# A scale from sums of the weights in place of a maximum over the products, its reduction first on GpSimd, and four early score blocks in place of eight

## The chip, the cores and the metric

The kernel runs on one core of one Trainium2 chip. The metric is the device time of one execution in microseconds (us); runs of one kernel agree within about 0.1% here (three runs before: 1170.21 to 1171.33). In the profile PE is TensorE (PEld its weight loads), DVE is VectorE, ACT is ScalarE, POOL is GpSimd and SP is SyncE, whose queue issues most DMAs. Each engine works through its own instructions in order.

## The reference

Two branches are added to a residual. With xn the layer norm of x (2048 tokens, 512 features):

```
A: y = Re(DFT_seq(DFT_hidden(xn)))          # dense DFT matrices, given as inputs
B: q  = xn @ w_q                            # 32 heads, two halves of 128 each
   s1 = q1 @ k1.T ; s2 = q2 @ k2.T          # 64 keys each
   top 2 of s1, top 2 of s2 -> 4 candidate sums -> top 2, softmax g
   act = gelu(xn . u[expert])               # 4096 experts
   out = sum g * act * v[expert]
result = x + A(xn) + B(xn)
```

The kernel never forms q. It multiplies w_q with the keys first (the "key products" M, one matrix of 512 x 512 for each chunk of four heads, eight chunks), and then xn with M to get the scores.

## The kernel before, in words

The program is written with a tile framework whose scheduler sets the order of instructions on each engine from the program order, its own costs and the dependencies. Buffers come from pools with a fixed number of slots; a tile in a reused slot waits until the last reader of the slot is done.

**Opening (up to about 90 us).** The tokens come in four groups of 512, in the order G = 1, 0, 2, 3. For each group `ln` (L328 to L367) computes the statistics and normalises, `fold` (L400 to L404) adds tokens that the DFT's symmetry pairs, giving Q[0][g], and `main(0, g)` (L435) multiplies it with a part of the DFT matrix into four PSUM banks of the tag `pa`. These are the "main sums". `evict(0)` (L487, L490) copies the four banks out on ACT, one row of the input (row 512, tile x5, handled on POOL by L367 and `fold_row`, `spread`, L409 to L422) entering as the bias s5c. Then `fold(1, g)` and `main(1, g)` do the second main sum in the same four banks, in the order 0, 1, 2, 3. `stage` (L503 to L505) splits the normalised tokens into two float16 parts and transposes them by DMA, through three staging slots. `sides` (L440 to L473) does some vectors on DVE and POOL.

**The key products of chunk 0** are made in the same stretch. `m_mul` (L148) multiplies w_q's chunk with the keys in float32, in two batches, into the banks `pc` and `pb`. `m_scale` (L187 to L212) then reads the four product tiles on ACT for sums of absolute values, two more sums over one tile of w_q and over the keys, reduces the three numbers over the partitions on POOL (`pow2`, L118, PARTITION_ALL_REDUCE) and makes powers of two from them on DVE: the scale of M[0] (L206, L207), and those of w_q, of the keys and of later chunks. `m_parts` (L219 on ACT, L220 on DVE) writes M[0] as a high and a low float16 part. With it `early(b)` (L266 to L271) computes score blocks: a score block is 128 tokens x 512 scores, 12 matmuls (`s_mm`, L245). Blocks 0 to 3 of the order TO (tokens of group 1) come after `main(0, 0)`, blocks 4 to 7 (tokens of group 0) after `main(1, 1)`; the first four are copied to SBUF (L271), the others stay in the four banks of `pb` and `pc`.

**Score stage.** For each chunk j and each of 16 token blocks `scores` runs the block (unless it is there already), copies it to a slot `ss` (four slots, L817 on ACT), and takes the top values and their places on DVE (L821, L825). Amid it the next chunk's M is built: the loads of chunk 1's w_q are issued by POOL (`m_load`, L134), and their first slots lie in memory that the opening has used; `m_prep` splits each tile in two float16 parts (L158, L163 on ACT; L166 on POOL or L160 on DVE), and stages 1 to 6 of `m_stage` multiply and split it at the blocks that MST0 (chunk 0) and MST name. `m_fit` (L185) sums the absolute values of a finished M for a check at the end. `sums` and `y_rows` (L509 to L521) finish the DFT's hidden side.

**Expert stages.** The rest of the time goes to the products with u (L945) and v (L1028) and what selects and weighs them (L973 to L999), with checks of the inputs beside them and a verdict at the end.

At the very start POOL makes an identity matrix, two iotas and three converted tables from them (`ident`, `iof`, `io_lam`, `io_c`, `hoff`, L72 to L104), which later stages read.

Of the kernel before, what the change touches and what calls it, by code (L numbers as in the profile page):

```python
# [19 lines left out]
P = 128  # L20
# [15 lines left out]
def tile_fnet_peer(ctx, tc, x, ca, cb, c5, wt, wf, wr, wq, kt, ut, vn, out):  # L36
# [33 lines left out]
    cst = ctx.enter_context(tc.tile_pool(name="cst", bufs=1))  # L70
    ident = cst.tile([P, P], F32, name="ident")
    make_identity(nc, ident)  # L72
    io_lam = cst.tile([P, P], F16, name="io_lam")
    io_c = cst.tile([P, NC], F16, name="io_c")
    with tc.tile_pool(name="iop", bufs=1, side="right") as iop:
        iof = iop.tile([P, P], F32, name="iof")
        nc.gpsimd.iota(iof, pattern=[[1, P]], base=0, channel_multiplier=0,
                       allow_small_or_imprecise_dtypes=True)
        nc.gpsimd.tensor_copy(io_lam, iof)
        nc.gpsimd.tensor_scalar(io_c, iof[:, :NC], float(P), None, op0=ALU.mult)  # L80
    eps = cst.tile([P, 1], F32, name="eps")
# [6 lines left out]
    nc.vector.memset(one, 1.0)  # L88
    nc.gpsimd.tensor_scalar(not0, ident[:, 0:1], -1.0, 1.0, op0=ALU.mult, op1=ALU.add)
    flag = cst.tile([1, 1], I32, name="flag")  # L90
    NW = 4 * (NCH - 1)
    NF = NW + 32 + NCH - 1
    sums_sb = cst.tile([P, 139 + NF + 3], F32, name="sums")
    chk, asum = sums_sb[:, 0:71], sums_sb[:, 71:139]


    wsc = cst.tile([P, 5], F32, name="wsc")
    sw, sk, smx, inv1 = wsc[:, 0:1], wsc[:, 1:2], wsc[:, 2:3], wsc[:, 3:4]
# [15 lines left out]

    def pow2(mx, pool, name, w=1):

        m = pool.tile([P, 4, w], F32, tag=f"pow2_{w}", name=name, bufs=2 if w == 1 else 1)
        nc.gpsimd.partition_all_reduce(m[:, 0], mx, P, bass_isa.ReduceOp.absmax)  # L118
        nc.vector.tensor_scalar(m[:, 1], m[:, 0], 1e-30, None, op0=ALU.max)
# [48 lines left out]
    def m_stage(j, pool, stage):  # L168

        if stage == 0:  # L170
            m_load(j, pool, range(4))
        elif stage < 5:
            m_mul(j, stage - 1, range(KD))
        elif stage == 5 and (j, 0, "h") in MS:
            M[j] = MP[j % 2].tile([P, 2, KD, 512], F16, tag="m", name=f"m{j}"), inv1
            MS[j, "s"] = smx
            if j > 1:
                m_fit(j - 1, M[j][0])
        elif stage == 5:
            m_scale(j, MS[j, "p"])  # L180
        else:
            m_parts(j, MS[j, "p"])

    def m_fit(j, junk):
        nc.scalar.activation(junk[:, 0], M[j][0][:, 0], AF.Abs, accum_out=fits[:, NW + 31 + j:NW + 32 + j])  # L185

    def m_scale(j, pm, at=None):  # L187

        if at is not None:
            nc.vector.tensor_copy(at, one)  # L190
        mp = MP[j % 2]
        w = 1 if at is None else 3
        mx = mp.tile([P, KD + w], F32, tag="mx" if w == 1 else "mx3", name=f"mx{j}")
        m = mp.tile([P, 2, KD, 512], F16, tag="m", name=f"m{j}")
        for kd in range(KD):
            nc.scalar.activation(m[:, 0, kd, :], pm[kd], AF.Abs, scale=1.0 if at is None else at,
                                 accum_out=mx[:, kd:kd + 1])
        if w == 3:
            nc.scalar.activation(m[:, 0, 0:2].rearrange("p k n -> p (k n)"),
                                 MS[j, 3].rearrange("p h k -> p (h k)"), AF.Abs, accum_out=mx[:, KD + 1:KD + 2])  # L200
            nc.scalar.activation(m[:, 0, 0, 0:P], k_sb.rearrange("p w k -> p (w k)"), AF.Abs,
                                 accum_out=mx[:, KD + 2:])
        nc.vector.tensor_reduce(mx[:, KD:KD + 1], mx[:, :KD], axis=AX.X, op=ALU.max)
        p, q = pow2(mx[:, KD:], mp, f"pw{j}", w)
# [3 lines left out]
        if w == 3:  # L208
            nc.vector.tensor_scalar(wsc[:, 0:2], q[:, 1:3], 2.0 ** 12, None, op0=ALU.mult)
            nc.vector.scalar_tensor_tensor(wsc[:, 4:5], p[:, 1:2], 2.0 ** -26, p[:, 2:3], op0=ALU.mult, op1=ALU.mult)  # L210
            nc.vector.scalar_tensor_tensor(smx, q[:, 0:1], 2.0 ** 11, wsc[:, 4:5], op0=ALU.mult, op1=ALU.mult)
            nc.vector.tensor_scalar(inv1, p[:, 0:1], 2.0 ** -12 / XS, None, op0=ALU.mult)  # L212
        M[j] = m, sc[:, 1:2]
        MS[j, "s"] = sc[:, 0:1]

    def m_parts(j, pm):
# [362 lines left out]
    for g in GK[1]:  # L579
# [64 lines left out]
    def part_b(safe, stS, stP, stE, xt, u_sb, cmp_p):  # L644
# [825 lines left out]
```

## Time and profile before

| what | value |
|---|---|
| median of three runs | 1170.43 us (1170.21 to 1171.33) |
| the profiled execution | 1170.59 us |
| its span, first to last instruction | 1168.8 us |
| PE busy | 1133.7 us (97%) |
| DVE busy | 934.9 us (80%) |
| ACT busy | 607.4 us (52%) |
| POOL busy | 247.8 us (21%) |
| mean granted TensorE clock | 0.988 |

A line of the time line has the start in us, the length, engine, source line, operation, output <- inputs with their shapes, the number of instructions merged into it, and in square brackets how long the engine stood idle before it and what ended that ("issue": nothing that the profile shows). A line of the waits has who waited for whom, the total in us, how often, and the longest. A line of a group has the total time, the mean of one in ns, and the idle time before. Float32 matmuls appear twice in the counts of PE.

### The profile page before, as it was taken

How to read it: one execution, taken by the hardware profiler on the slowest of the kernel's cores; microseconds unless marked ns; L12 is line 12 of the kernel's file. 1: busy time of each engine (PE TensorE's matmuls, PEld its weight loads, DVE VectorE, ACT ScalarE, POOL GpSimd, SP SyncE). 2: the span in 40 equal slices, each digit the busy share in tenths (PEclk: the TensorE clock that was granted, in tenths of full speed). 3: DMA queues.
4: the chain of work that ended last, by engine and by line, in shares of the span. 5: the costliest groups of instructions: out<-in, count | busy, mean ns of one | idle time of the engine just before them, and what ended most of it. 6: DMA issues, size and time to landing. Idle time of an engine off the chain costs nothing.

```text
span 1168.8 us, 25265 instructions
## 1 busy us (share of the span) xinstructions
PE 1133.7 (97%) x9858; PEld 720.1 (62%) x9858; DVE 934.9 (80%) x2848; ACT 607.4 (52%) x1050; POOL 247.8 (21%) x235
## 2 busy tenths in 40 slices
PE   5598999999999999999999999999999999999997
PEld 4244655445445449868469569569559659658763
DVE  7698788798898999983995886787886887788670
ACT  5537667777776754353535436535535436434440
POOL 5222636757757330000010010010000000000000
PEclk9798899999999999999999999999999999999999
DMA  9477055342341203260643644545545455442423
GB/s 338 123 168 265 31 173 177 109 163 91 108 160 40 91 26 109 84 223 11 213 171 130 200 155 158 184 158 171 178 161 176 166 171 167 154 154 68 142 73 103
DMA packets 98400, 167.83 MB, mean 144 GB/s; under 512 B 32980, under 2 KB 48219, under 8 KB 98270
## 3 DMA queue, kind: packets, MB, share of 16 engines
q1 hardware_dynamic: 97328, 163.94, 43.1%
q0 software_dynamic: 640, 2.10, 0.5%
q8 instruction: 79, 1.29, 0.5%
q14 instruction: 51, 0.42, 0.1%
q10 hardware_dynamic: 302, 0.08, 0.0%
HBM read 142.69 MB, written 17.63 MB: 137 GB/s over the span
## 4 chain that ended last, share of the span: by engine, by line
PE 75%; DVE 15%; POOL 4%; issue 2%; DMA 2%; ACT 1%; POOLq 0%; SPq 0%; DVEq 0%; ACTq 0%
PE v L1028 27%; PE z L945 26%; PE s L245 15%; PE g L983 4%; DVE vals L821 4%; DVE idx L825 3%; PE m L144 1%; PE p L435 1%; POOL wq L165 1%; DVE L L973 1%; POOL wq L166 1%; DVE z L763 1%; DVE act L999 1%; DMA wq<-in_wq_dram 1%; DVE ft L400 1%
## 5 line engine op out<-in xcount | busy, mean ns | idle before, releaser
L945 PE MATMUL z<-xb,u 128*128 128x256 f16 (+1 forms) x3840 | 342.7, 251 | 0.0
L1028 PE MATMUL v<-v,act 128*128 128x512 f16 x1536 | 338.6, 379 | 0.0
L945 PEld LDWEIGHTS <-u 128*128 128x128 f16 x3840 | 309.4, 98 | 26.8
L245 PE MATMUL s<-m,xq 128*128 128x512 f16 x1344 | 301.7, 383 | 11.8 <-DVE m L220 11.8
L1028 PEld LDWEIGHTS <-act 128*128 128x128 f16 x1536 | 147.1, 98 | 171.2
L245 PEld LDWEIGHTS <-xq 128*128 128x128 f16 x1344 | 130.5, 99 | 166.0 <-issue 17.8
L973 DVE TENSOR_TENSOR L<-io_lam,cmp 128x2048 f16<-128x2048 f16 x128 | 155.9, 1218 | 59.2 <-PE g L983 59.0
L952 ACT ACTIVATE act<-z,scl 128x256 f32<-128x256 f32 (+1 forms) x224 | 100.8, 498 | 169.2 <-PE z L945 169.1
L1041 POOL TENSOR_TENSOR y<-y,xr 128x512 f32<-128x512 f32 x15 | 25.3, 1685 | 613.7 <-DMA y<-y_d 393.5
L821 DVE MAX8 vals<-ss 128x8 f32<-128x64 f32 x896 | 133.5, 217 | 5.0 <-ACT ss L817 4.7
L998 ACT ACTIVATE act<-w 128x1024 f16<-128x1024 f32 x52 | 69.9, 1361 | 96.5 <-DVE w L991 95.9
L991 DVE SCALAR_TENSOR_TENSOR w<-act,scl,g 128x1024 f32<-128x1024 f32 x64 | 81.0, 1274 | 29.7 <-ACT act L952 29.7
L817 ACT ACTIVATE ss<-s,wsc 128x512 f32<-128x512 f32 x112 | 74.8, 681 | 49.6 <-PE s L245 42.8
L1104 ACT ACTIVATE cx<-cx 128x896 f32<-128x896 f32 x64 | 60.5, 946 | 69.9 <-DVE cx L1084 51.6
L825 DVE FIND_INDEX8 idx<-vals,ss 128x8 uint16<-128x256 f32 x224 | 93.9, 419 | 0.0
L999 DVE TENSOR_TENSOR act<-w,act 128x1024 f16<-128x1024 f32 x64 | 85.3, 1335 | 4.2 <-ACT act L998 4.2
L983 PEld LDWEIGHTS <-L 128*128 128x128 f16 x2048 | 60.7, 96 | 11.7 <-DVE R L981 1.2
L1078 DVE TENSOR_TENSOR cx<-cx 128x512 f32<-128x512 f32 (+2 forms) x84 | 48.4, 610 | 22.7 <-DMA cx<-in_cb_dram 22.6
L983 PE MATMUL g<-R,L 128*128 128x32 f16 x2048 | 61.9, 177 | 0.7 <-DVE R L981 0.6
L981 DVE TENSOR_TENSOR R<-R,cmp 128x512 f16<-128x512 f16 x128 | 59.9, 468 | 1.5
L166 POOL TENSOR_TENSOR wq<-wq,wh 128x1024 f16<-128x1024 f32 x26 | 55.4, 2131 | 11.4 <-ACT wq L163 10.4
L978 DVE TENSOR_TENSOR R<-io_c,cmp 128x512 f16<-128x512 f16 x128 | 54.6, 426 | 0.0
(299 smaller groups left out, 1114.0 us busy)
## 6 DMA issues: line engine op xcount, KB each, us to landing
v<-v_d SPq DMA_DIRECT2D x67, 512.0 KB, 3.8
cx<-in_cb_dram SPq DMA_DIRECT2D x64, 448.0 KB, 4.6
wq<-in_wq_dram SPq DMA_DIRECT2D x28, 512.0 KB, 4.8
fit<-in_wq_dram SPq DMA_DIRECT2D x28, 512.0 KB, 5.1
uv<-in_vn_dram SPq DMA_DIRECT2D x16, 512.0 KB, 3.6
uv<-in_ut_dram SPq DMA_DIRECT2D x16, 512.0 KB, 3.6
c<-in_ca_dram SPq DMA_DIRECT2D x8, 512.0 KB
y<-y_d SPq DMA_DIRECT2D x16, 256.0 KB, 3.1
```

What stands on the lines that cost most here:

```text
L245: nc.tensor.matmul(ps, xt[i][:, l, kd, :], m[:, r, kd, :], start=(n == 0), stop=(n == 3 * KD - 1))
L817: nc.scalar.activation(s, ps, AF.Copy, scale=inv)
L821: nc.vector.max(vals[:, i, w, :, h], s[:, g, :])
L825: nc.vector.max_index(idx[:, i, w].rearrange("p k h -> p (k h)"), vals[:, i, w, 0:2].rearrange("p k h -> p (k h)"), s[:, w * HC:g + 1, :]. ...
L945: nc.tensor.matmul(ps if n == 1 else ps.rearrange("p (b n) -> p b n", b=2), ug[:, l, c % 2, kd, :], xb2[:, k0, r, kd, :] if n == 1 else xb ...
L952: nc.scalar.activation(ACT[bb][:, cg * m:cg * m + m, :], pv[:, i], AF.Gelu_apprx_tanh, scale=zsc)
L973: nc.vector.tensor_tensor(L.rearrange("p t (l two) -> p t l two", two=2), io_lam.rearrange("p (l two) -> p l two", two=2).unsqueeze(1).to_ ...
L983: nc.tensor.matmul(p[:, hf, t * NC:(t + 1) * NC], L[:, t, :], R[:, t, :], start=True, stop=True)
L991: nc.vector.scalar_tensor_tensor(w, act[:, :, ts], fw, p.rearrange("p h (n c) -> p c (h n)", c=NC), op0=ALU.mult, op1=ALU.mult)
L998: nc.scalar.activation(w16[..., 0], w, AF.Copy)
L999: nc.vector.tensor_tensor(w16[..., 1], w, w16[..., 0], op=ALU.subtract)
L1028: nc.tensor.matmul(pv, w16[:, c, :, l], v_sb[g][:, r, cc, :], start=(n + cc == 0 and k == 0), stop=(n == 15 and cc == 1 and k == 2))
```

## The change

The scale of M[0] is no longer taken from the products but from the weights: the sum of absolute values over one tile of w_q times that over the keys. So `m_scale` is not used for chunk 0. A new `w_sums` runs its two passes on ACT in the first group's step, as soon as the first tile of w_q and the keys are there, and a new `w_scale` reduces the two numbers over the partitions and makes all scales from them on DVE; it stands in the second group's step, ahead of `fold(0, 0)`, and is tied to that group's rstd by its lower bound `low`. The reduction is now POOL's first larger instruction: identity, iotas and tables at the start are gone, one iota and three conversions come behind the reduction, and the identity's one use (`not0`) is a pair of memsets on DVE. In the order on POOL the reduction stands after four memsets and the copy of two elements of c5r, ahead of the normalising of row 512; the iota and the conversions stand amid the row work.

`m_parts` for chunk 0 keeps its place in the program. In the built order its four steps on ACT and DVE stand amid the fold of the second group and the statistics of the fourth. `early` is called for four blocks only; blocks 4 to 7 of TO become ordinary blocks of the score stage, and in the built order on PE they follow `main(1, 3)` directly, where before they lay between `main(1, 1)` and `main(1, 2)`. They now use the `pa` banks. Stages 1 to 6 of the second chunk's M come one block earlier in the order of blocks, `m_fit` is also done for chunk 0, and later chunks get the constant 2^-11 as scale. The copy zs[:, 1], which orders later stagings, is taken from the fourth group's rstd.

```diff
-    ident = cst.tile([P, P], F32, name="ident")
-    make_identity(nc, ident)
...
-    with tc.tile_pool(name="iop", bufs=1, side="right") as iop:
-        iof = iop.tile([P, P], F32, name="iof")
-        nc.gpsimd.iota(iof, pattern=[[1, P]], base=0, channel_multiplier=0,
-                       allow_small_or_imprecise_dtypes=True)
-        nc.gpsimd.tensor_copy(io_lam, iof)
-        nc.gpsimd.tensor_scalar(io_c, iof[:, :NC], float(P), None, op0=ALU.mult)
...
-    nc.gpsimd.tensor_scalar(not0, ident[:, 0:1], -1.0, 1.0, op0=ALU.mult, op1=ALU.add)
+    nc.vector.memset(not0, 1.0)
+    nc.vector.memset(not0[0:1], 0.0)
...
-    nc.gpsimd.iota(hoff, pattern=[[64, HC]], base=0, channel_multiplier=0,
-                   allow_small_or_imprecise_dtypes=True)
...
-    def pow2(mx, pool, name, w=1):
+    def pow2(mx, pool, name, w=1, r=None, low=1e-30):
...
-            MS[j, "s"] = smx
-            if j > 1:
-                m_fit(j - 1, M[j][0])
+            MS[j, "s"] = 2.0 ** -11
+            m_fit(j - 1, M[j][0])
...
+    def w_sums():
+        m = MP[0].tile([P, 2, KD, 512], F16, tag="m", name="m0")
+        mx = MP[0].tile([P, 2], F32, tag="mx", name="mx")
+        nc.scalar.activation(m[:, 0, 0:2].rearrange("p k n -> p (k n)"),
+                             MS[0, 0].rearrange("p h k -> p (h k)"), AF.Abs, accum_out=mx[:, 0:1])
+        nc.scalar.activation(m[:, 0, 2, 0:P], k_sb.rearrange("p w k -> p (w k)"), AF.Abs, accum_out=mx[:, 1:2])
+        M[0] = m, inv1
+        MS[0, "s"] = sm0
+        return mx
+
+    def w_scale(mx, low):
+        with tc.tile_pool(name="iop", bufs=1, side="right") as iop:
+            iof = iop.tile([P, P], F32, name="iof")
+            p, q = pow2(mx, MP[0], "pw", 2, iof[:, 0:2], low)
+            nc.gpsimd.iota(iof, pattern=[[1, P]], base=0, channel_multiplier=0,
+                           allow_small_or_imprecise_dtypes=True)
+            nc.gpsimd.tensor_copy(io_lam, iof)
+            nc.gpsimd.tensor_scalar(io_c, iof[:, :NC], float(P), None, op0=ALU.mult)
+            nc.gpsimd.tensor_scalar(hoff, iof[:, :HC], 64.0, None, op0=ALU.mult)
+        nc.vector.tensor_scalar(wsc[:, 0:2], q, 2.0 ** 12, None, op0=ALU.mult)
+        nc.vector.scalar_tensor_tensor(sm0, q[:, 0:1], 2.0 ** 13, q[:, 1:2], op0=ALU.mult, op1=ALU.mult)
+        nc.vector.scalar_tensor_tensor(inv1, p[:, 0:1], 2.0 ** -15 / XS, p[:, 1:2], op0=ALU.mult, op1=ALU.mult)
...
+        if n == 1:
+            nc.vector.tensor_scalar(wsc[:, 0:1], rstd[:, g, 0:1], 0.0, 1e-15, op0=ALU.mult, op1=ALU.add)
+            w_scale(wmx, wsc[:, 0:1])
         fold(0, g)
+        if n == 0:
+            wmx = w_sums()
...
         if n == 3:
+            nc.scalar.activation(zs[:, 1:2], rstd[:, G[3], 0:1], AF.Copy, scale=0.0)
             fold_row(0)
...
         if n == 1:
-            m_scale(0, MS[0, "p"], FF[0, g][:, 0, 0:1])
             m_parts(0, MS[0, "p"])
-            nc.scalar.activation(zs[:, 1:2], wsc[:, 0:1], AF.Copy, scale=0.0)
...
         main(1, g)
-        if g == 1:
-            for b in range(4, 8):
-                early(b)
...
-        MST0 = MST if safe else {10: 1, 11: 2, 12: 3, 13: 4, 14: 5, 15: 6}
+        MST0 = MST if safe else {9: 1, 10: 2, 11: 3, 12: 4, 13: 5, 14: 6}
```

More of the change, by code (lines that the diff above doesn't have):

```diff
@@ L5 @@
 from concourse import bass_isa, mybir
-from concourse.masks import make_identity
 from concourse._compat import with_exitstack
@@ L88, in tile_fnet_peer @@
     nc.vector.memset(one, 1.0)
-    nc.gpsimd.tensor_scalar(not0, ident[:, 0:1], -1.0, 1.0, op0=ALU.mult, op1=ALU.add)
+    nc.vector.memset(not0, 1.0)
+    nc.vector.memset(not0[0:1], 0.0)
     flag = cst.tile([1, 1], I32, name="flag")
     NW = 4 * (NCH - 1)
-    NF = NW + 32 + NCH - 1
+    NF = NW + 32 + NCH
     sums_sb = cst.tile([P, 139 + NF + 3], F32, name="sums")
     chk, asum = sums_sb[:, 0:71], sums_sb[:, 71:139]
-    wsc = cst.tile([P, 5], F32, name="wsc")
-    sw, sk, smx, inv1 = wsc[:, 0:1], wsc[:, 1:2], wsc[:, 2:3], wsc[:, 3:4]
+    wsc = cst.tile([P, 4], F32, name="wsc")
+    sw, sk, sm0, inv1 = wsc[:, 0:1], wsc[:, 1:2], wsc[:, 2:3], wsc[:, 3:4]
     k16 = sums_sb[:, 0:128].bitcast(F16).rearrange("p (l w k) -> p l w k", l=2, w=2)
@@ L113, in tile_fnet_peer @@
     su, sv = usc[:, 1:2], usc[:, 4:5]
-    def pow2(mx, pool, name, w=1):
+    def pow2(mx, pool, name, w=1, r=None, low=1e-30):
         m = pool.tile([P, 4, w], F32, tag=f"pow2_{w}", name=name, bufs=2 if w == 1 else 1)
-        nc.gpsimd.partition_all_reduce(m[:, 0], mx, P, bass_isa.ReduceOp.absmax)
-        nc.vector.tensor_scalar(m[:, 1], m[:, 0], 1e-30, None, op0=ALU.max)
+        r = m[:, 0] if r is None else r
+        nc.gpsimd.partition_all_reduce(r, mx, P, bass_isa.ReduceOp.absmax)
+        nc.vector.tensor_scalar(m[:, 1], r, low, None, op0=ALU.max)
         nc.vector.tensor_scalar(m[:, 2].bitcast(I32), m[:, 1].bitcast(I32), 0x7F800000, None,
@@ L184, in m_fit, with m_scale @@
     def m_fit(j, junk):
[L185 to L190, printed above, removed]
+        nc.scalar.activation(junk[:, 0], M[j][0][:, 0], AF.Abs, accum_out=fits[:, NW + 32 + j:NW + 33 + j])
+    def m_scale(j, pm):
         mp = MP[j % 2]
-        w = 1 if at is None else 3
-        mx = mp.tile([P, KD + w], F32, tag="mx" if w == 1 else "mx3", name=f"mx{j}")
+        mx = mp.tile([P, KD + 1], F32, tag="mx", name=f"mx{j}")
         m = mp.tile([P, 2, KD, 512], F16, tag="m", name=f"m{j}")
         for kd in range(KD):
[L196 to L202, printed above, removed]
+            nc.scalar.activation(m[:, 0, kd, :], pm[kd], AF.Abs, accum_out=mx[:, kd:kd + 1])
         nc.vector.tensor_reduce(mx[:, KD:KD + 1], mx[:, :KD], axis=AX.X, op=ALU.max)
-        p, q = pow2(mx[:, KD:], mp, f"pw{j}", w)
+        p, q = pow2(mx[:, KD:], mp, f"pw{j}")
         sc = mp.tile([P, 2], F32, tag="msc", name=f"msc{j}")
@@ L207, in m_scale @@
         nc.vector.tensor_scalar(sc[:, 1:2], p[:, 0:1], 2.0 ** -14 / XS, None, op0=ALU.mult)
[L208 to L212, printed above, removed]
         M[j] = m, sc[:, 1:2]
         MS[j, "s"] = sc[:, 0:1]
+    def w_sums():
[19 more added lines that the diff above has]
+        nc.vector.scalar_tensor_tensor(inv1, p[:, 0:1], 2.0 ** -15 / XS, p[:, 1:2], op0=ALU.mult, op1=ALU.mult)
     def m_parts(j, pm):
```

## The prediction

> **What bounds the kernel now.** I read the page first, then the table of waits of TensorE, then the time line engine by engine over the first 130 us, then the table of stretches for busy time and granted clock.
>
> ```profile
> span 1168.8 us, 25265 instructions
> PE 1133.7 (97%) x9858; PEld 720.1 (62%) x9858; DVE 934.9 (80%) x2848; ACT 607.4 (52%) x1050; POOL 247.8 (21%) x235
> ...
> PE s L245 <- DVE m L220: 11.8, 1, 11.8
> PE m L148 <- DMA wq<-in_wq_dram: 9.2, 1, 9.2
> PE m L144 <- POOL wq L166: 3.2, 1, 3.2
> ```
>
> PE is busy for all but 35 us of the span, and these three waits, all in the first 101 us, are 24 of them. So a time is won or lost here as PE idles less or more there, or as PE runs at a lower clock there. The table of stretches shows both (its columns: the stretch and its length, then the busy time of PE, PEld, DVE, ACT and POOL with the number of instructions, the granted clock, the DMA share, GB/s), and that nothing behind absorbs a shift: from 140 to 440 us PE is never idle.
>
> ```profile
> 28.10:33.10 5.00, 5.00 (x8) 2.05 (x9) 3.85 (x11) 4.48 (x12) 4.86 (x8) 0.72 1.00 234
> 32.00:42.50 10.50, 1.15 (x3) 0.29 (x2) 0.06 (x1) 3.21 (x9) 4.10 (x5) 0.77 0.11 34
> 42.50:72.70 30.20, 27.30 (x87) 11.73 (x87) 29.82 (x86) 18.22 (x34) 0.00 (x0) 0.91 0.72 185
> 71.30:81.80 10.50, 10.50 (x50) 4.93 (x49) 10.50 (x27) 1.44 (x2) 4.76 (x1) 1.00 0.35 101
> 96.40:100.20 3.80, 0.24 (x4) 0.14 (x3) 2.40 (x17) 3.80 (x8) 2.12 (x1) 0.86 1.03 409
> 100.20:106.20 6.00, 6.00 (x34) 2.90 (x35) 5.39 (x27) 3.51 (x8) 2.12 (x1) 0.52 0.92 346
> 140.00:440.00 300.00, 300.00 (x1906) 147.20 (x1904) 273.54 (x1435) 212.07 (x323) 169.64 (x156) 1.00 0.33 111
> ```
>
> From 32.0 to 42.5 us DVE does 0.06 us of work and PE 1.15. The time line of POOL, ACT, DVE and PE (in that order below) says why.
>
> ```profile
> 10.63 0.24 POOL L77 IOTA iof<- 128x128 f32 x1 [9.70 <-issue]
> ...
> 17.42 4.21 POOL L367 TENSOR_SCALAR x<-x,mvs,rstd 1x512 f32<-1x512 f32 x2 [3.58 <-DVE rstd L351]
> ...
> 34.93 0.87 POOL L422 DMA_DIRECT2D s5c<-s_d  x1
> 42.09 0.40 POOL L118 PARTITION_ALL_REDUCE pw<-mx  x1 [6.28 <-issue]
> ...
> 89.34 2.33 POOL L134 DMA_DIRECT2D wq<-in_wq_dram  x4 [5.15 <-ACT u L487]
> 98.02 2.12 POOL L166 TENSOR_TENSOR wq<-wq,wh 128x1024 f16<-128x1024 f32 x1 [6.34 <-ACT wq L163]
> ...
> 11.95 0.63 ACT L328 ACTIVATE q<-xb 128x512 bf16<-128x512 f32 x1 [1.13 <-DMA xb<-in_x_dram]
> ...
> 16.22 0.30 ACT L347 ACTIVATE sm<-mvs,eps 128x4 f32<-128x4 f32 x1 [0.87 <-DVE mvs L343]
> ...
> 33.69 0.20 ACT L201 ACTIVATION_READ_ACCUMULATOR m<-k_sb 128x1 f32 x1
> ...
> 62.36 1.58 ACT L490 ACTIVATE u<-p,s5c 128x256 f32<-128x256 f32 x4
> ...
> 95.57 1.15 ACT L158 ACTIVATE wh<-wq,ss 128x1024 f16<-128x1024 f32 x1 [2.81 <-DMA wq<-in_wq_dram]
> ...
> 17.55 0.22 DVE L354 TENSOR_SCALAR nm<-negm,not 128x2 f32<-128x2 f32 x1
> ...
> 22.31 1.22 DVE L349 SCALAR_TENSOR_TENSOR ff<-mvs,ff 128x4 f32<-128x4 f32 x1
> ...
> 27.92 0.41 DVE L404 TENSOR_TENSOR q<-fo 128x257 f32<-128x257 f32 x1
> ...
> 42.52 0.17 DVE L119 TENSOR_SCALAR pw<-pw 128x3 f32<-128x3 f32 x1 [10.46 <-POOL pw L118]
> ...
> 44.09 2.73 DVE L220 SCALAR_TENSOR_TENSOR m<-m,msc,m 128x512 f16<-128x512 f32 x4
> 46.74 0.34 DVE L575 SCALAR_TENSOR_TENSOR sums<-k_sb,wsc,sums 128x128 f16<-128x128 f32 x1
> ...
> 72.25 0.41 DVE L404 TENSOR_TENSOR q<-fo 128x255 f32<-128x255 f32 x1
> ...
> 80.51 1.87 DVE L504 TENSOR_TENSOR u<-xq,u 128x512 f16<-128x512 f32 x3
> ...
> 21.83 3.68 PE L148 MATMUL m<-k_sb,wq 128*128 128x64 f32 x32
> 28.05 5.09 PE L435 MATMUL p<-c,q 128*128 128x512 f32 x8 [2.55 <-DVE q L403]
> 44.90 12.02 PE L245 MATMUL s<-m,xq 128*128 128x512 f16 x48 [11.75 <-DVE m L220]
> ...
> 81.61 7.03 PE L435 MATMUL p<-c,q 128*128 128x512 f32 x16
> ...
> 101.36 5.04 PE L245 MATMUL s<-m,xq 128*128 128x512 f16 x12
> ```
>
> The sums that the maximum needs are there at 33.9 us. POOL is then still on the row work that began at 17.42 and ends at 35.8, and 6.28 us in which the profile shows nothing follow before the reduction runs at 42.09; POOL's first use of an iota has the same mark, 9.70 us. DVE stands behind the reduction for 10.46 us, and PE behind DVE for 11.75.
>
> **The change, part by part.** The sum is made up to the point at which eight score blocks and all of both main sums are done: 88.64 us before (81.61 + 7.03).
>
> *Reduction first on POOL.* Removed ahead of it: identity, iotas, casts; they return behind it. It now follows a 1x2 copy of c5r, which ACT's queue brings. By 9 us all that ACT's queue moves has landed: the page's count for that queue, and the DMA view of 0 to 9 us:
>
> ```profile
> q10 hardware_dynamic: 302, 0.08, 0.0%
> ...
> q10 hardware_dynamic: 302, 0.08, 4.1%
> ```
>
> The silent time before the reduction I bound by its two rows: 6.28 gives a reduction at about 15, 9.70 one at about 18.5. I take 9.70, nearest in place (both fall into the first 20 us), and keep both ends. [...]
>
> DVE asks for the result behind L354, at 17.8. So it waits 0 to 1 us; I take 0.7, and DVE goes on at 18.5. ACT's new passes are a short one over k before the first square root and one over 128x1024 of w_q (1.15 for that size, row 95.57, and 0.2 for its sum) ahead of the second group's statistics. ACT stood idle there for 1.13 before 11.95 and for 0.87 before 16.22, on DVE: the 1.4 fits, nothing on the path.
>
> *Scale and parts of M[0] inside the second group's fold.* DVE had Q[0][0] at 28.3. Ahead of it now come the wait (0.7), some seven small scale steps (42.52 to 44.09, less one copy of 0.62: 0.9) and three of four part steps (2.73 x 3/4 = 2.0); the stretched small step of 22.31 (1.22, where its like of the same 128x4 in 42.52 takes 0.17) lay beside POOL's row work, which now comes later, so I take off 1.2. Q[0][0] comes at about 30.7, the last part of M[0] at about 32.3 (k's low part 0.34, one part 0.68, one statistic that I put at as much). PE's second product batch ends at 25.5 as before, so PE idles 5.2 instead of 2.55, and the first main sum of 5.1 to 5.5 (0.72 clock, as at 28.10) ends at 36.0. M is ready by then, and the four early blocks start at once: 10.4 at full clock, to 46.4. The 11.75 is gone.
>
> *Main sums without a gap.* Six main-sum steps are left, 3.5 each (16 rows in 7.03): 21.1. Ahead of the second sum ACT must copy the PSUM banks out (row 62.36, 0.4 each); I put 0.7 for it. PE ends both sums at 46.4 + 21.1 + 0.7 = 68.2. The four blocks that lay between them now follow: 10.5, to 78.7. Against 88.64 this is **-9.9**. DVE has to feed it: from 42.52 to 72.66 it had 30.1 us of work nearly without a pause. Of these the scale, parts and k (0.9 + 2.73 + 0.34) have been done, and what it did from 28.3 to 32.0 (3.7) is still to come: 29.8, from 32.3 to 62.1, nearer 60 as some scans of early blocks move behind. PE takes the last Q at 64.7. Cover of 2.5 to 5 us; if it is gone each us costs one.
>
> *What was held by the reduction on POOL.* Normalising of row 512, its folds and s5c now follow reduction, a second silent time (6.28 to 9.70) and 2.5 us of iota and casts (POOL's time line from 10.63 to 13.1): 18.9 + 6.3 + 18.4 + 2.5 = 46.1, at worst 49.5; I put 3 for its way, so 49 to 52. The folded row is wanted by DVE near 48.5 (it is ready 4 us ahead of s5c's issue), s5c by ACT at 53. Hidden; when late, ACT's copy-out is what stands still. The later silent time ahead of the first wide step on POOL falls away, where it cost nothing (POOL waited for DVE there).
>
> *Products of the second chunk.* Its loads are issued on POOL when the second sum's banks are out: 89.34 before, right after ACT's last copy; now about 69.4. First w part on ACT 6.2 later: 75.7 (before 89.34 to 95.57). ACT by then has the last staging copies and a new pass over M[0] (128x2048, so twice 1.15) ahead of it, so I put it at 78.6, the low part on POOL (98.02 row, 2.12) at 83.1. PE comes to it after blocks 8 and 9, at 78.7 + 5.2 = 83.9. The gap of 3.17 + 0.4 goes: **-3.6**; and the 0.52 clock behind it (the 101.36 row: 5.04 for a block of 2.6; 6.0 us at 0.52) goes: **-2.9**. But the second tile's low part is DVE's, and it stands behind the scans of nearly nine blocks. From the page, 112 blocks:
>
> ```profile
> L821 DVE MAX8 vals<-ss 128x8 f32<-128x64 f32 x896 | 133.5, 217 | 5.0 <-ACT ss L817 4.7
> ...
> L825 DVE FIND_INDEX8 idx<-vals,ss 128x8 uint16<-128x256 f32 x224 | 93.9, 419 | 0.0
> ```
>
> That is 2.0 a block, a little less in time since the records overlap. DVE: 60, side sums 7.9 (72.66 to 80.51), six staging copies 3.7 (1.87 for three), 8.8 blocks at 1.8 to 2.0 16 to 18, the step itself 1.3: 89 to 91. I take 89.6, against PE's 87.3, a new gap: **+2.3**, with an even chance of another slow stretch, half of 2.9: **+1.4**.
>
> *Four early blocks fewer.* The PE work is the same 10.4, moved; DVE and ACT do the same copies and scans. One more pass of 2.3 us on ACT (52% busy): nothing but the place above.
>
> Sum: -9.9 - 3.6 - 2.9 + 2.3 + 1.4 = -12.7. The profiled execution took 1170.59 (span 1168.8), 0.16 above the median of 1170.43; the sum against it gives 1157.9.
>
> [...] After 2.55 us of idle PE still had 0.72 over the next 5, and after 3.6 only 0.52 over 6. [...]
>
> **The rivals.**
> - *DVE takes over* (faster, but by 2.4 to 8): POOL's row work now lies beside the fold steps. Where it did before, a step of 0.16 took 1.22 (row 22.31). If 8 to 10 of DVE's steps between 32 and 62 lose 1 us each, the cover of 2.5 to 5 is spent and PE loses the rest, some 5; with blocks 0 to 3 moved behind the sums PE has nothing to fill it with. 1162 to 1166. Against it: from 17.55 to 28.3, beside that work, DVE lost little more than the one step.
> - *The change doesn't do what it says* (no change): the reduction comes as late as before because its load waits for full DMA queues. It would have to come at 28 or later, 19 us after the copy, against rows of 6.28 and 9.70. About 1170.
> - *Slower*: s5c. ACT takes instructions in order, and its first copy-out (L490) needs s5c. With both sums' banks shared, PE's second main sum can't start before it, and no score block is left in between. It decides when s5c lands 12.7 us after PE needs it, that is at about 66 instead of 49 to 52: POOL's row work would have to take twice its 18.4. Then 1171 to 1177. Nothing in the rows shows such a factor over the whole chain.
>
> **How the numbers follow.** The forecast (8 to 18 faster) gets 0.70, DVE or ACT taking over part of it 0.17, no change 0.05, slower 0.08. The forecast's own range is 1152 to 1162.5; to hold eight in ten I reach into the next case, to 1167. 0.2%, 2.3 us, is what a measurement of this kernel can tell from none. Faster 0.87, same 0.05, slower 0.08.
>
> **What would show it.** Right: the reduction at 15 to 18.5, DVE's wait for it under 1 us; PE's first score block near 36 with no wait for M[0]; the main sums done near 68; the wait of the second chunk's products for POOL gone, one of about 2 for DVE in its place. Wrong: a wait of PE for DVE's Q or for ACT's copies between 36 and 68 of more than 5 in all, or s5c as the releaser of ACT's first copy-out.

## The result, and the profile after

The changed kernel takes 1163.12 us (median of four runs, 1162.19 to 1164.22) against 1170.81 beside it (1170.21 to 1171.33): a ratio of 0.9935, interval 0.9918 to 0.9952. The profiled execution took 1162.19, 8.4 less than the one of before. The forecast was 1157.9 with a range of 1152 to 1167: faster, as forecast, but by 8 where 12.7 was worked out. The median lies 0.6 above the 1152 to 1162.5 that the prediction gives to its own sum; it is in the wider range only by the part of a rival's range that was added to it.

The agreement of about 0.1% named at the start is that of three runs. Over all runs here the spread is wider: the kernel before took 1169.06 to 1174.79 in 25 of them, and single variants of the changed kernel spread by up to 0.5%. So a difference of 2 or 3 us between the medians of two variants says little by itself; the traces have to show where it lies.

The page and TensorE's waits of the kernel after, over the first 140 us (who waited for whom, total, times, longest):

```profile
span 1160.3 us, 25236 instructions
PE 1130.8 (97%) x9858; PEld 720.7 (62%) x9858; DVE 936.4 (81%) x2846; ACT 606.4 (52%) x1045; POOL 249.1 (21%) x232
...
PE m L139 <- DMA wq<-in_wq_dram: 9.1, 1, 9.1
PE p L438 <- issue: 4.6, 1, 4.6
PE p L438 <- DVE q L406: 4.3, 1, 4.3
PE b L605 <- DVE m L223: 3.8, 1, 3.8
PE m L135 <- DVE wq L151: 0.6, 1, 0.6
```

The wait of 11.8 for M[0] and that of 3.2 for GpSimd's part are gone. In their place are one of 4.6 without a named releaser and one of 3.8 for a part step of DVE; neither was in the forecast at that size. The time line of PE, POOL, ACT and DVE (in that order) of the kernel after shows where each lies:

```profile
28.34 5.28 PE L438 MATMUL p<-c,q 128*128 128x512 f32 x8 [4.25 <-DVE q L406]
33.45 10.52 PE L248 MATMUL s<-m,xq 128*128 128x512 f16 x48
43.81 7.03 PE L438 MATMUL p<-c,q 128*128 128x512 f32 x16
55.44 15.66 PE L438 MATMUL p<-c,q 128*128 128x512 f32 x32 [4.60 <-issue]
...
70.94 5.34 PE L248 MATMUL s<-m,xb 128*128 128x512 f16 x24
76.12 10.52 PE L248 MATMUL s<-m,xq 128*128 128x512 f16 x48
...
104.05 3.58 PE L605 MATMUL b<-w,u 128*128 128x2 f32 x16 [3.84 <-DVE m L223]
...
155.62 0.39 PE L512 MATMUL hy<-u,u 128*128 128x129 f32 x2
...
7.59 0.17 POOL L541 COPY c<-c5r 1x2 f32<-1x2 f32 x1 [6.67 <-DMA c5r<-in_cb_dram]
11.72 0.38 POOL L109 PARTITION_ALL_REDUCE iof<-mx  x1 [3.96 <-DMA xb<-in_x_dram]
22.63 5.35 POOL L370 TENSOR_SCALAR x<-x,mvs,rstd 1x512 f32<-1x512 f32 x2 [10.53 <-DVE ff L351]
...
42.38 0.87 POOL L425 DMA_DIRECT2D s5c<-s_d  x1
...
75.19 2.16 POOL L125 DMA_DIRECT2D wq<-in_wq_dram  x4 [3.09 <-issue]
...
11.44 0.19 ACT L198 ACTIVATION_READ_ACCUMULATOR m<-wq 128x1 f32 x1
...
71.14 0.60 ACT L490 ACTIVATE u<-p 128x512 f32<-128x512 f32 x1 [0.26 <-PE p L438]
...
17.58 0.23 DVE L110 TENSOR_SCALAR pw<-iof,wsc 128x2 f32<-128x2 f32 x1
...
74.63 0.69 DVE L507 TENSOR_TENSOR u<-xq,u 128x512 f16<-128x512 f32 x1 [0.59 <-ACT u L506]
```

The reduction is there at 12.1, before DVE asks for it. The early blocks follow the main sum of the second group at 33.45 without a wait. Eight blocks and both sums are done where half of the 48 rows from 76.12 are: 76.1 + 5.3 = 81.4, against 88.6 before: -7.2. From there to the fifth product with 128 rows of the DFT's hidden side the gain grows by only 1.0. It stands at 155.62 here and in the kernel before at the second of these rows:

```profile
116.44 1.95 PE L601 MATMUL b<-w,u 128*128 128x2 f32 x16 [0.39 <-DVE m L220]
...
163.85 0.39 PE L509 MATMUL hy<-u,u 128*128 128x129 f32 x2
```

That is -8.2, which is nearly all of the 8.5 by which the spans differ; behind it nothing is won or lost. What makes the 1.0 is a ledger. The first product's wait falls from 3.17 + 0.40 to nothing, and that of a later one rises to 0.6: -3.0. The wait for DVE ahead of the hidden side's sums (L601, now L605) rises from 0.39 to 3.84: +3.4. The rest is the clock. One stretch of the kernel before, and then three of the kernel after (the columns are those of the prediction, the granted clock third from the end):

```profile
119.60:126.50 6.90, 6.90 (x32) 5.09 (x32) 3.02 (x16) 2.42 (x14) 6.90 (x3) 0.51 0.01 1
```

```profile
28.10:31.50 3.40, 3.16 (x4) 1.51 (x5) 3.40 (x7) 2.48 (x7) 3.32 (x9) 0.50 1.09 205
55.40:58.80 3.40, 3.36 (x4) 1.51 (x5) 3.40 (x8) 2.97 (x6) 0.00 (x0) 0.51 1.07 252
103.20:113.50 10.30, 9.46 (x41) 7.23 (x42) 5.00 (x20) 2.91 (x10) 5.72 (x3) 0.50 0.00 0
```

Past 90 us the kernel before had 6.0 us at 0.52 and 6.9 at 0.51, that is 6.3 us of lost clock (an estimate: busy time times the share of the clock that is missing). The kernel after has 10.3 at 0.50, 9.46 of them busy, 4.7 lost: -1.6. Together -3.0 + 3.4 - 1.6 = -1.2, near the 1.0.

### The profile page after: what moved, and what is told of

It reads as the page before. It is cut to its first block, busy times and chain, and to the rows that moved or that the text cites. A ratio compares the mean times of both kernels' runs of the same rounds, so it can differ in the third digit from the quotient of the medians.

```text
span 1160.3 us, 25236 instructions
## 1 busy us (share of the span) xinstructions
PE 1130.8 (97%) x9858; PEld 720.7 (62%) x9858; DVE 936.4 (81%) x2846; ACT 606.4 (52%) x1045; POOL 249.1 (21%) x232
## 3 DMA queue, kind: packets, MB, share of 16 engines
q8 instruction: 79, 1.29, 0.5%
## 4 chain that ended last, share of the span: by engine, by line
PE 87%; DVE 8%; DMA 3%; issue 1%; ACT 1%; POOL 0%; SPq 0%; ACTq 0%; DVEq 0%; POOLq 0%
PE z L949 28%; PE v L1032 26%; PE s L248 26%; PE g L987 4%; PE m L135 1%; DVE ft L403 1%; DMA wq<-in_wq_dram 1%; DVE L L977 1%; DVE u L507 1%; DMA u<-in_vn_dram 1%; DMA cx<-in_wt_dram 1%; DVE u L445 0%; DVE ff L382 0%; DMA x<-in_x_dram 0%; DVE act L1003 0%
## 5 line engine op out<-in xcount | busy, mean ns | idle before, releaser
L248 PE MATMUL s<-m,xq 128*128 128x512 f16 x1344 | 298.1, 380 | 0.0
L821 ACT ACTIVATE ss<-s,wsc 128x512 f32<-128x512 f32 x124 | 83.0, 680 | 52.0 <-PE s L248 44.3
L157 POOL TENSOR_TENSOR wq<-wq,wh 128x1024 f16<-128x1024 f32 x26 | 55.9, 2150 | 11.3 <-ACT wq L154 10.3
```

The lines of the kernel that those rows point to most:

```text
L248: nc.tensor.matmul(ps, xt[i][:, l, kd, :], m[:, r, kd, :], start=(n == 0), stop=(n == 3 * KD - 1))
L821: nc.scalar.activation(s, ps, AF.Copy, scale=inv)
```

## The experiments

All ratios are to the kernel before, run beside it on the same chip; the changed kernel's own is 0.9935 (0.9918 to 0.9952), and 0.1% is 1.2 us. What a trace shows is that of one run.

**Four early blocks alone, in the kernel before.**

```diff
         main(1, g)
-        if g == 1:
-            for b in range(4, 8):
-                early(b)
...
-        MST0 = MST if safe else {10: 1, 11: 2, 12: 3, 13: 4, 14: 5, 15: 6}
+        MST0 = MST if safe else {9: 1, 10: 2, 11: 3, 12: 4, 13: 5, 14: 6}
```

> The kernel before with that part alone: four early blocks instead of eight and the second chunk's steps one block earlier; scale and reduction as before. Theory: no gain, since TensorE still stands 11.75 us ahead of the first blocks; the second chunk's first product comes at 100 us as before with one score block less done, so 1171 to 1174. Rival: the move of the blocks is the gain: 1163 to 1166.

1175.43 us, ratio 1.0036 (1.0024 to 1.0048). The wait for M[0] stays (11.1), and TensorE now also waits 3.8 for DVE's part step at L598, as in the changed kernel. So this part of the change costs some 4 us by itself, 1.4 more than the top of the theory's range, and the new wait is its mark.

**Eight early blocks, in the changed kernel** (the same edit the other way round).

> The changed kernel with one part undone: eight early blocks again (blocks 4 to 7 of the order between the second and third step of the second main sum), and the second chunk's steps at the old places. Theory: the early blocks are the same TensorE work at another place, so the gap ahead of the second main sum stays (4 to 5 us) and the time is within 2 us of the changed kernel (1161 to 1165). Rival: the move of the four blocks itself brought the gain; then the time goes back to 1167 to 1171.

1161.98 us, ratio 0.993 (0.9907 to 0.9954): as fast as the changed kernel. The gap ahead of the second main sum stays, at 3.3. The 3.84 falls to 0.40, but the wait for GpSimd's part of the second chunk is back at 3.2, since the loads are issued at 80.02 and not at 75.19. In the changed kernel the move of the four blocks is a swap of one wait for the other, and not the gain.

**Iota and tables first on POOL again, in the changed kernel.**

```diff
+    with tc.tile_pool(name="iop0", bufs=1, side="right") as iop0:
+        iof0 = iop0.tile([P, P], F32, name="iof0")
+        nc.gpsimd.iota(iof0, pattern=[[1, P]], base=0, channel_multiplier=0,
...
         with tc.tile_pool(name="iop", bufs=1, side="right") as iop:
             iof = iop.tile([P, P], F32, name="iof")
             p, q = pow2(mx, MP[0], "pw", 2, iof[:, 0:2], low)
-            nc.gpsimd.iota(iof, pattern=[[1, P]], base=0, channel_multiplier=0,
```

> The changed kernel with the iota, its tables and hoff at the very start of GpSimd again, ahead of the reduction. Theory: the first iota comes at 10.6 us as in the kernel before, the reduction follows the conversions and a silent time of 4 to 6 us, at 17 to 19 us instead of 11.7; VectorE waits 0 to 2 us for it at 17.6; row 512's work starts when its own silent time is over, at 26 to 29 instead of 22.6, s5c is issued at 44 to 47 instead of 42.4, still ahead of the copy-out at 54.5. Time 1163 to 1165. Rival: being first on GpSimd is what the gain hangs on: VectorE waits over 5 us and the time is 1167 or more.

1167.66 us, ratio 0.997 (0.9959 to 0.9981). The time line of POOL, DVE and PE (in that order) in this run:

```profile
9.32 0.24 POOL L74 IOTA iof<- 128x128 f32 x1 [8.89 <-issue]
...
20.02 0.37 POOL L117 PARTITION_ALL_REDUCE iof<-mx  x1 [9.42 <-issue]
30.75 4.44 POOL L373 TENSOR_SCALAR x<-x,mvs,rstd 1x512 f32<-1x512 f32 x2 [10.37 <-DVE q L409]
...
20.42 0.23 DVE L118 TENSOR_SCALAR pw<-iof,wsc 128x2 f32<-128x2 f32 x1 [2.58 <-POOL iof L117]
...
30.70 6.39 PE L441 MATMUL p<-c,q 128*128 128x512 f32 x8 [6.02 <-DVE q L409]
```

The silent time is paid twice in a row ahead of the reduction, 8.89 and 9.42; the reduction comes 8.3 later than in the changed kernel, DVE then stands 2.58 behind it, and the run is 0.35% (4 us) slower than the changed kernel. The time is the rival's, though DVE's wait is only half of the rival's 5 us. The trace has the 4 us ahead of the score blocks: TensorE stands 6.02 ahead of the second group's main sum where it stood 4.25, that sum takes 6.39 and not 5.28, the gap ahead of the second sum is 5.2 and not 4.6, and the 48 rows of score blocks begin at 80.46 and not at 76.12. So of the 0.65% that the change gives, 0.35% hangs on the reduction being first on POOL. The other 0.3% is what the rest of the change gives with the iota first; no run has the scale from the weights without that rest.

**The copy-out ahead of the ninth staging copy.** This run and the next are about the 4.60 without a releaser. ACT's time line of the kernel after, at that place:

```profile
53.88 0.72 ACT L506 ACTIVATE u<-xq,zs 128x512 f16<-128x512 f32 x1 [3.58 <-DMA xq<-u]
54.51 1.57 ACT L493 ACTIVATE u<-p,s5c 128x256 f32<-128x256 f32 x4
```

The copy-out (L493), for which TensorE waits, stands in ACT's order behind a staging copy (L506) that waits 3.58 for a transpose to give back one of the three staging slots. s5c had been asked for at 42.38, landed 3.8 us later and is not the cause. The first edit ties the stagings from the ninth on behind `evict(0)`, by a bias that the evicted data gives:

```diff
-        nc.scalar.activation(t[:, 0], src, AF.Identity, bias=zs[:, int(n > 3):int(n > 3) + 1])
+        nc.scalar.activation(t[:, 0], src, AF.Identity, bias=zs[:, int(n > 3) + int(n > 7):int(n > 3) + int(n > 7) + 1])
...
     evict(0)
+    nc.scalar.activation(zs[:, 2:3], PT[0][1][1][:, 0:1], AF.Copy, scale=0.0)
```

> The changed kernel, with stagings 8 and later tied behind the first copy-out of the banks on ACT (their bias is a zero made from the last copied bank), so that ACT copies the banks out before it takes staging copies 8 and 9. Theory: TensorE's gap of 4.60 us at 50.9 (it stands ahead of the second main sum) comes from ACT, which had staging copy 9 in front of the copy-out and waited 3.58 us there for the transpose that frees its slot. Then the gap falls to 1 us or less and the time from about 1163 to 1159 to 1160. Rival 1: the copy-out waits for the bias s5c from GpSimd; then the gap stays above 3 us and the time within 1 us of 1163. Rival 2: the gap goes, but what is gained is lost again where the sums wait for VectorE (3.84 us at 100.2 in the changed kernel): time within 1.5 us of 1163, that wait 6 to 8 us.

1165.76 us, ratio 0.9957 (0.9945 to 0.9969): no faster than the changed kernel, and slower by the median, though the intervals touch. The gap is gone, as PE's time line of this run shows: ACT's order was its cause. But ACT's last four staging copies now come at 73.56, the first of them after this wait:

```profile
45.54 20.76 PE L438 MATMUL p<-c,q 128*128 128x512 f32 x48
...
73.56 0.72 ACT L506 ACTIVATE u<-xq,zs 128x512 f16<-128x512 f32 x1 [6.63 <-DMA xq<-u]
```

They stand ahead of the copies of score blocks, and TensorE waits 3.6 for those (ss, L822); the second chunk's loads are issued at 80.01 and 2.6 for GpSimd's part and 4.1 for DVE's follow. The gain is given back behind, and more than that: as the second rival had it, but at other places than the sums, whose wait is 4.1 and not 6 to 8.

**Five staging slots.**

```diff
-        t = u_sb[3 + n % 3 // 2][:, n % 3 % 2].rearrange("p a k n -> p a (k n)")
+        ug, uh = ((3, 0), (3, 1), (4, 0), (12, 1), (14, 1))[n % 5]
+        t = u_sb[ug][:, uh].rearrange("p a k n -> p a (k n)")
```

> The changed kernel with five staging slots instead of three; nothing else. Theory (the 4.6 us gap ahead of the second main sum is ACT's ninth staging copy, which stands in front of the copy-out and waits for a transpose to give its slot back): the gap (main sum with releaser 'issue', 4.60 at 55.44) falls below 1.5 us, the last staging copy is done some 4 us earlier (74.6 before), so the loads of the second chunk are issued near 70 instead of 75.19, and the wait of TensorE for the part steps (3.84) stays or grows to at most 6. Time 1157 to 1161. Rival (the transposes' DMA queue itself is the limit, not the number of slots): the gap stays above 3 us and the time stays within 1 us of 1163. Second rival, as with the tied stagings: the gap goes and comes back as a wait behind; 1163 to 1166.

1168.71 us, ratio 0.9971 (0.996 to 0.9981). The gap falls to 0.9, so the slots were its cause; both sums are done at 67.7, 3.4 earlier. Yet the run is 0.36% (4 us) slower than the changed kernel: the second rival had the kind, a wait that comes back behind, and not the size. TensorE's waits in this run, and the time lines of SP, POOL and ACT:

```profile
PE m L135 <- ACT wh L149: 5.7, 1, 5.7
PE m L135 <- DVE wq L151: 2.6, 2, 1.6
PE b L606 <- DVE m L223: 2.3, 1, 2.3
...
73.45 13.58 SPq L509 DMA_TRANSPOSE xq<-u  x4
...
90.82 0.63 SPq L671 DMA_DIRECT2D u<-in_vn_dram  x1
...
73.28 2.16 POOL L125 DMA_DIRECT2D wq<-in_wq_dram  x4 [0.30 <-POOL u L476]
...
98.42 1.15 ACT L675 ACTIVATE u<-u,ss 128x1024 f32<-128x1024 f32 x1 [10.20 <-DMA u<-in_vn_dram]
99.56 1.13 ACT L149 ACTIVATE wh<-wq,ss 128x1024 f16<-128x1024 f32 x1
```

The last four transposes hold SP's queue for 13.58 here, where the single one at 60.30 in this run held it for 1.29: the second chunk's loads (four of 512 KB) start at the same time, at 73.28, and one of v of the same size at 73.01. The transposes are through at 87.03; two more loads and four copies follow them on SP's queue, and the load of v behind those goes out at 90.82 instead of 86.59. ACT waits 10.20 for it with its pass over v, and behind that pass in ACT's order stands the fourth tile's part (L149, wh), for which TensorE waits 5.7.

**The passes over u and v two blocks later.**

```diff
-            for which, n in ((0, 8), (1, 10)):
+            for which, n in ((0, 8), (1, 12)):
...
-            todo[11].append(lambda at: uv_scale())
+            todo[13].append(lambda at: uv_scale())
```

The changed kernel has the same knot, smaller. Its chain of work that ended last (start, length, what), here from the second chunk's loads to the part step:

```profile
76.31 8.12 DMA wq<-in_wq_dram
...
85.33 1.04 ACT wh L149
...
86.59 7.11 DMA u<-in_vn_dram
...
95.03 1.05 ACT wh L149
...
96.10 1.28 DVE wq L151
97.39 0.65 DVE u L825 x5
...
103.41 0.59 DVE m L223
```

> The changed kernel with the two blocks' passes over u and v (the check of the inputs: absolute sum over v and the scale made from it) put two steps later among the score blocks, so that ACT has no pass that waits for v's load ahead of its part of the second chunk's fourth tile. Theory (the wait of TensorE for DVE's part step, 3.84 us at 100.2, comes from the fourth tile's first part on ACT, which stood behind that pass and its 3.64 us wait for the load): the wait falls below 1.5 us, time 1159 to 1161. Rival (the part steps are late because DVE has scans and staging behind it): the wait stays at 3 to 4.5 and the time within 1.5 us of 1163.

1160.28 us, ratio 0.9904 (0.9881 to 0.9928). The wait at L605 falls to 2.7, less than the theory had, and ACT no longer waits for v ahead of the fourth tile. What is left of the wait is DVE, which comes to the part step (L223) at 101.76, behind scans and with no wait of its own:

```profile
101.76 0.67 DVE L223 SCALAR_TENSOR_TENSOR m<-m,m 128x512 f16<-128x512 f32 x1
```

So the 3.84 had both causes, ACT's wait for about a third and DVE's scans for two thirds. The time came out where the theory had it, but by luck, and its interval overlaps the changed kernel's. TensorE's waits behind the blocks come to 5.3 here (1.6 for GpSimd's part and 1.0 for DVE's beside the 2.7) against 4.4 in the changed kernel, and most of the lead of this run lies ahead of the blocks:

```profile
54.81 13.97 PE L438 MATMUL p<-c,q 128*128 128x512 f32 x32 [2.99 <-issue]
...
73.80 10.52 PE L248 MATMUL s<-m,xq 128*128 128x512 f16 x48
```

The 48 rows begin at 73.80 and not at 76.12, and the fifth product with 128 rows of the hidden side at 152.93 and not at 155.62: 2.3 of 2.7 us are won where the edit changes nothing. Up to there both kernels have the same instructions in the same order on every engine; the gap is 2.99 and no half clock follows (the 32 rows take 13.97), where the changed kernel's profile had 4.60 and 3.4 us at half (15.66).

**Both edits.**

> Both of the two edits before: five staging slots, and the passes over u and v two steps later. If each works by its own theory the gains add: 1154 to 1158, with neither the gap of 4.6 nor the wait of 3.84. If the earlier loads only bring the next wait (for DVE's low part of the second tile, or for the part steps behind the scans), the time is 1158 to 1162. If the transposes are the limit, it is the time of the run with the later passes alone.

1163.22 us, ratio 0.9934 (0.9914 to 0.9955). The wait for the fourth tile's part (5.7 with five slots alone) is gone, and with it 5.5 us: so the pass over v was what the five slots had lost. (Here the traces agree: the 48 rows begin at 72.67 and 72.60, the fifth product at 161.06 and 155.80.) But the transposes still take 13.16 for four, the wait at L606 is 5.4, and the time lies above all three expectations: nothing is won against the changed kernel.

**Eight early blocks and five slots.**

> The changed kernel with eight early score blocks, as the kernel before had them, and five staging slots. With eight early blocks alone the time was 1161.98, with a gap of 3.3 us ahead of a main sum and a wait of 3.2 us for GpSimd's part of the second chunk. Theory (both stand behind the staging slots): both fall below 1.5 us, time 1156 to 1159. Rival (they stand behind the transposes' queue): both stay and the time stays at 1161 to 1163.

1159.19 us, ratio 0.9896 (0.9878 to 0.9914), the lowest median of all. Its interval just misses the changed kernel's, and overlaps that of the later passes alone. SP and POOL in this run:

```profile
69.13 6.66 SPq L509 DMA_TRANSPOSE xq<-u  x4
...
78.39 2.16 POOL L125 DMA_DIRECT2D wq<-in_wq_dram  x4 [5.67 <-ACT u L490]
```

With the four blocks back between the sums, the second sum's banks are copied out later, the loads go out at 78.39, and the four transposes are through by 75.8, in half the time they take beside the loads. The gap ahead of the second main sum is 1.5 in two pieces, and the wait at L609 0.3. The theory was only half right: the wait for GpSimd's part (3.2) stays, since it hangs on those later loads. That the collision is the cause is read from four traces (two with the loads issued within 0.2 us of the transposes, 13.58 and 13.16; two with the loads behind them, 6.66 and 6.48), and not shown by moving the loads alone.

**Three more combinations.** The same edits, with eight early blocks: all three, and without the five slots. And the changed kernel with the former block numbers of the second chunk's steps (10 to 15) alone.

> The changed kernel with eight early blocks, five staging slots and the passes over u and v two steps later. If the three edits add as they did in pairs, this takes 1156 to 1159, at or below the 1159.2 of the run without the later passes. If what is left there (3.2 us for GpSimd's part of the second chunk) is all that is left, the later passes change nothing: 1158.5 to 1160.

1162.36 us, ratio 0.9922 (0.9903 to 0.9941). The waits are nearly those of the run before (3.8 for GpSimd's part in place of 3.2, 0.3 at L609), and its profiled span, 1157.2, is within 1.2 of that one's: the later passes have nothing left to win here. The median is above both expectations; what the 3 us are isn't shown.

> The changed kernel with eight early blocks and the passes over u and v two steps later, three staging slots as in the change. With eight early blocks alone it was 1161.98, with both edits and five slots it is expected at 1156 to 1159. If the slots matter in this order too, it takes 1160 to 1163 with the gap of some 3.3 us ahead of a main sum still there; if only the later passes matter, it takes as long as the run with all three edits.

1161.76 us, ratio 0.9909 (0.9885 to 0.9932). With three slots the gap ahead of the main sum is back, at 4.4.

> The changed kernel with the steps of the second chunk at the block numbers of the kernel before (10 to 15 in place of 9 to 14); four early blocks as in the change. Theory (the wait of 3.84 us for DVE's part step comes from steps that ask for the fourth tile's parts one block, 2.6 us, earlier than they can be there): the wait falls to 1 to 2 us, but TensorE's products find their operands with time to spare, time 1160 to 1162. Rival (the parts move later with the step numbers, since DVE and ACT take them in the same order): the wait stays between 3 and 5, time 1162 to 1165.

1162.33 us, ratio 0.9927 (0.9904 to 0.995). The wait at L605 grows to 5.6, against the theory and past the rival: the four products end later, DVE's part step with them (104.23), and the tile `b` in `sums`, which keeps its place, waits so much longer for its bank of `pc`. The time is that of the changed kernel within the interval: no product waits any more, and this run too had the shorter gap ahead of the second sum, 2.7 without a half clock behind it (32 rows in 13.97), with the same instructions up to there.

## Why the prediction was right, and where it was not

- *The reduction first.* Put at 15 to 18.5, measured at 11.72, and DVE's wait for it at 0.1 instead of 0.7. The size was wrong, on the safe side: the silent time is at most 4.0 here (7.76 to 11.72), below both rows that I bounded it by. What the reduction waited for last was ACT's sum over w_q, ready at 11.63: here it starts 0.1 behind that sum, and in five further profiles with this order on POOL (tied stagings, eight early blocks alone, with the later passes and with all three edits, the former block numbers) it starts between 11.78 and 12.25 with that sum named as what it waited for last. So the silent time was over by then and its own length stays open. The reduction ends at 12.1 and DVE asks at 17.5, so over 5 us of slack were left; the iota run, in which the reduction comes at 20.02 and the time is 4 us worse, shows what is lost when they are used up.
- *Q[0][0] at 30.7, first block at 36.0.* Measured 28.6 and 33.45, with 4.25 of idle instead of 5.2. The three part steps do stand ahead of it, 0.74 each as summed, so the term that was too large is the rest: 0.6 of it is the wait; DVE also came to this place 0.35 earlier (17.33 against 17.68), and the steps of the fold that had been stretched before by some 2.1 in all, of which I took off 1.2, were stretched by 0.4. The main sum took 5.28, within the 5.1 to 5.5 given.
- *The 11.75 goes.* Right: no wait for M at the first block, early blocks done at 43.9.
- *0.7 for the copy-out ahead of the second main sum.* **This is the step that failed.** It measured 4.60 in the profile. I priced the copies by their own length and took s5c as all that could hold them; the rival for that place was s5c too, and it was asked for at 42.38 and landed 3.8 later, well in time. What held them was another instruction ahead of them in ACT's order, a staging copy waiting for a slot; the tied stagings remove the gap and the five slots leave 0.9 of it. The half clock behind it (3.4 us at 0.51) took another 1.7 (32 rows in 15.66; in the runs without it 13.97). So both sums ended at 71.1 and not at 68.2, although the stretch had begun 2.5 early. The size is not a fixed one: four more profiles have the same instructions up to this gap (eight early blocks, the later passes, both of these, the former block numbers), and there it measured 3.3, 3.0, 4.4 and 2.7. A half clock followed the 4.6 and the 4.4 (behind the 4.4, 16 rows took 8.80, against 7.10 behind the 3.3) and none of the others. The term of 0.7 was too small in all five; that the loss was as much as 5.6 is the changed kernel's profile.
- *-9.9 at eight blocks.* Measured -7.2, by that step.
- *The second chunk's loads at 69.4.* They went at 75.19. My bound was ACT's last copy of the second sum, and that was done at 71.7; the last staging copy on DVE, at 74.63 to 75.3, was later. In the six profiles with four early blocks and three slots the loads go out 0.4 to 0.6 after that copy begins. The price of it was small: the low part was there at 85.6, and TensorE came to it at 86.5. -3.6 forecast, -3.6 measured (3.17 + 0.40, both gone).
- *+2.3 at the second product, for DVE behind the scans.* 0.6 came, and at the fourth. The same lateness struck at a place for which the sum has no term: `sums` takes a bank that the products hold until DVE's part step. That is the 3.84. The run with four early blocks in the old kernel shows it with the same 3.8.
- *Clock.* -2.9 + 1.4 = -1.5 forecast, -1.6 measured past 90 us, though in another place: behind `sums`, not behind the second product. That the two agree is luck.
- *The sum.* 12.7 forecast; 2.7 of it fell at the copy-out, net of the earlier start, and 3.4 at `sums`, and 1.7 came back (the second product's 2.3 that wasn't, less the 0.6), together 4.4, near the 4.3 between 1157.9 and 1162.19. This adds up for the profiled run; in another run of the same instructions the part at the copy-out can be over 2 us smaller, as the gaps above show.
- *Rivals.* No rival came true as written. The nearest is the first, by its size (1162 to 1166): ACT, not DVE, stood still, over a slot and not over slow steps; the case "DVE or ACT taking over part of it", given 0.17, is where the median falls. The sign of being wrong that was named, over 5 us of waits for DVE's Q and ACT's copies between 36 and 68, came close with 4.60 and wasn't met.
- *The clock behind a gap.* The gaps of 4.25 and 4.60 are each followed by 3.4 us at half (0.50 and 0.51). In the kernel before the clock stood at 0.50 from 27.5 to 30.9, from inside the gap of 2.55 on, and behind the gaps of 3.0 and 3.3 ahead of the second sum it didn't fall (32 rows in 13.97, 16 in 7.10), so in these runs the length of the gap alone doesn't settle it.

## What to carry to other kernels

A copy that TensorE waits for can cost far more than its own length: here the 0.7 put for it became 4.60, as a staging copy ahead of it in ACT's order waited 3.58. So read the instructions in front of it and what each of them needs, a buffer slot above all. When early work is pulled forward, look for every tile whose buffer another chain must free, also those of side work (the bank that `sums` takes: 3.84); and before loads are started earlier, see which transfers they then share the time with: with five slots, and with both edits, four transposes beside the loads took 13.58 and 13.16, against 6.66 with the loads behind them, and the gain of the earlier start was given back one or two queues further on. And before a faster run is put down to an edit, see in the trace whether it is faster behind the edit or already ahead of it.

## What the runs showed of the hardware

The silent time that GpSimd spends ahead of a first reduction, or of the first work after one, isn't a constant in these runs. It was 6.28 before, at most 4.0 as the first larger instruction (the reduction then waited for its operand), 9.42 behind an iota; the row work after a reduction came 10.53 and 10.37 later, though a different releaser is named in each, and behind a later reduction of the kernel after it was this:

```profile
106.59 2.85 POOL L156 TENSOR_SCALAR wq<-wq,wsc 128x1024 f32<-128x1024 f32 x1 [7.64 <-issue]
```

So these rows go from 4.0 or less to about 10.5.

TensorE's granted clock stood at half for 3.4, 3.4 and 10.3 us in the stretches of the kernel after above, and in the kernel before, up to 140 us, for 3.4, 10.2, 6.8 and 6.8 (from 27.5, 37.7, 99.2 and 119.6). The 10.3 isn't idle time: in its 9.46 of busy time TensorE runs mostly float32 matmuls of 1, 2 or some 128 columns. The kernel before has its own half stretch, at 119.60, in the same work behind a wait of only 0.39.

The same instructions met the half clock in different ways: the second group's main sum took 5.28, 5.50, 5.74, 5.79, 5.98, 6.42 and 6.61 in seven profiles with this order on POOL, and the gap ahead of the second sum was followed by a half stretch at 4.60 and 4.36 and by none at 3.29, 2.99 and 2.72.

With five slots four transposes by DMA held SP's queue for 13.58, 3.4 each on average, while four loads of 512 KB and one of v were under way; the single one at 60.30 in that run held it for 1.29.
